# Spreading the scales 1/deviation by a turn on VectorE and transfers, and starting the seven-product form one chunk earlier

## The chip, the cores and the metric

The kernel runs on one core of a Trainium2 chip. The metric is the device time of one execution in microseconds. The kernel before has a median of 1026.7 us in three runs (1024.91, 1026.70 and 1027.67). PE is TensorE, DVE is VectorE, ACT is ScalarE, POOL is GpSimd, and SP only issues transfers.

## The reference, cut to what matters

```python
x = A_q                                            # 1 x 2048 x 576
xn = (x - mean(x)) / sqrt(var(x) + 1e-5)           # over the 576 channels
kv = v * (causal convolution of k with 4 taps)     # per channel
y = (causal convolution of kv with ssm_k, 2048 long) + kv * ssm_D
out = x + xn * y + relu(xn @ w1) @ w2              # w1: 576 x 4608, w2: 4608 x 576
```

The last term is the feed-forward part, and most of the work. The long convolution is done as a transform, a product and a transform back.

## The kernel before

**Chunks.** The feed-forward part takes the tokens in two halves of 1024, and in each half the 4608 hidden channels in 18 chunks of 256: 36 chunks in all, numbered g = 0 to 35. In a chunk the 1024 tokens are two blocks b = 0, 1 of 512, and the 256 hidden channels are two groups f = 0, 1 of 128. A chunk has a first part, relu(xn @ w1), which goes to the tiles psh, and a second part, which multiplies the hidden values of the chunk before by w2 in eight **units** (`open_unit` and `mm2`, 128 tokens each) into the tiles pso. There are two pso buffers, and a unit can only begin when DVE has added the unit before the last to acc (line 748 or 752). Each value is kept as a high and a low part (`hh` and `ll`, or index 0 and 1 of an operand) and a product is done as high times high, high times low and low times high: three matmuls for each 128 channels.

**Two forms of the first part.** In the plain form (`classical`) each of the four pairs (b, f) takes 12 matmuls for 512 of the 576 channels and two for the remaining 64: 56 matmuls of 128x512 per chunk. In the seven-product form (`quad`) sums of operands and of weights replace one of eight block products: seven products of six matmuls, and four times two for the remaining 64 channels, so 50. Its operands are called, in the order in which `quad` uses them, 00, 01, s2, s1, s3, s4 and 11; the remaining channels are hl0 and hl1. `PLAIN = 3`: chunks 0 to 2 are plain, chunk 3 is the first with seven products. In `quad` the order on PE is: product 00, units 0 and 1, product 01 and hl0, unit 2, s2, unit 3, s1, unit 4, s3, hl0, s4, units 5 and 6, hl1, unit 7, 11, hl1. After s4, DVE adds `u2` (line 686), ACT then refills a psh buffer (line 688), and the matmuls of hl1 wait for that.

**The start.** The plain chunks use operands that are centred but not divided by the deviation, and DVE multiplies a unit's result by rstd, which is 1/deviation (line 748). The seven-product chunks use operands that are already scaled. For them each block needs rstd as a row over its 512 tokens, the same on all 128 partitions (`row[b]`). The kernel before makes diagonal matrices from rstd on DVE (`diagonal`, eight instructions), multiplies them on PE by a matrix of ones (`scales`, line 327, one matmul in full float32 for each block) and copies the result out on ACT (line 330).

**Pieces.** With the rows there, `second_half_of_start` is a generator of pieces: `scaled` multiplies an operand by its row (line 340, DVE), `combined` takes differences of operands (line 227, DVE), and `made` splits an operand into its high part (line 212, ACT) and its low part (line 213, DVE). A piece is put into the program behind each unit (`post(1)`) and behind each `classical` (`post(3)`). The yields "00" and "10" are barriers, since the new operands overwrite those that the plain form still reads. If `quad` comes to an operand that isn't made yet, `need` puts the missing pieces there, right ahead of the product. `here()` orders a piece behind the newest addition to acc and the newest hh that were written before it.

**What sets the order.** PE follows the order in which its instructions are written. DVE and ACT run in one fixed order each, which a scheduler has set at build time within the orders that the code asks for; on the chip an engine does not pass over an instruction that waits. The long convolution's work is a second stream (`conv`), whose steps `tick` deals out between the feed-forward's matmuls by a budget: `rate` comes from `FFN_TOTAL`, which counts the chunks after the plain ones, and the stream begins when the pool of the start closes, after the first seven-product chunk. In its stage of products, a product reads psf on DVE (line 1051), sends parts through a transfer, and the next `join` (line 1063) waits for that transfer.

Of the kernel before, what the change touches and what calls it, by code (L numbers as in the profile page):

```python
# [10 lines left out]
F32 = mybir.dt.float32  # L11
F32R = mybir.dt.float32r
AF = mybir.ActivationFunctionType
OP = mybir.AluOpType
# [3 lines left out]
P = 128  # L18
# [28 lines left out]
W_MM = 512  # L47
W_UNIT = 2 * FT * 3 * NH
PAUSE = 16000
PLAIN = 3  # L50
PAUSES = 7.5
SHARE = 0.935

# [46 lines left out]
def h3_ffn_kernel(ctx: ExitStack, tc, x, k, v, shift_k, ssm_k, ssm_D, w1, w2, fwd, inv, mid, out):  # L100
# [27 lines left out]
    rows_n = dram.tile([HB, BT // 2, 2, P, D], F32, name="rows_n")  # L128
    ops_n = {o: dram.tile([P, 2, 2, 512], F32, name=f"ops_{o}") for o in OPERANDS}
    hl_n = dram.tile([HB, P, 512], F32, name="hl_n")  # L130

    def at_t(z, t):

# [6 lines left out]
    def fft_psum():  # L140
        return ps_f.tile([P, 512], F32, tag="f", name="psf")
# [170 lines left out]

    row = {}

    def diagonal(pool, b):
        diag = pool.tile([P, 2, D], F32, tag="xn", name=f"diag{b}", bufs=4)
        diag = diag[:, 0, :BT * P].rearrange("p (i n) -> p i n", i=BT)
        for i in range(BT):
            nc.vector.tensor_scalar(diag[:, i, :], ident, rstd[:, b * BT + i:b * BT + i + 1],
                                    None, op0=OP.mult)  # L320
        return diag

    def scales(pool, b, diag):

        ps = fft_psum()
        with tc.issue_after(done["pe"].ins):
            done["pe"] = nc.tensor.matmul(ps, ones, diag.rearrange("p i n -> p (i n)"),
                                          start=True, stop=True)
        row[b] = pool.tile([P, 512], F32, tag=f"row{b}", name=f"row{b}")
        nc.scalar.activation(row[b], ps, AF.Copy)  # L330

    def scaled(o, b):
        if isinstance(o, int):
# [18 lines left out]
    def made_rest(b):  # L352
        with here():
            split_rest(rest_operand(b), xf[b])
        ready.add(b)
        yield

    def combined(pool, o):
        for c in range(2):
            with here():  # L360
                combine(pool, xf, (o,), c)
            yield

    def second_half_of_start(pool):


        for o, b in (("11", 1), ("10", 1), ("00", 0), ("01", 0)):
            yield from scaled(o, b)
        for o in ("s1", "s2"):
            yield from combined(pool, o)  # L370
            yield from made(o)
        yield from combined(pool, "s3")
        yield from made("s3")
        yield from scaled(0, 0)
        yield "00"
        yield from made("00")
        yield from made("01")
        yield from made_rest(0)
        yield from combined(pool, "s4")
        yield from scaled(1, 1)  # L380
        yield "10"
        yield from made("s4")
        yield from made_rest(1)
        yield from made("11")
# [826 lines left out]
    load_acc(BT + 2)  # L1211
    for j in range(FT):
        load_w2(0, j)
    ones = const.tile([P, P], F32, name="ones")
    nc.vector.memset(ones, 1.0)
    table = const.tile([P, 1], F32, name="table")
    nc.vector.memset(table, 1.0)
    nc.scalar.activation(table, table, AF.Sqrt)
# [8 lines left out]
    with tc.tile_pool(name="fa", bufs=1) as fa:  # L1227
        block_xT(fa, 0, ("00", "01"), (None, None), block_rows(fa, 0))
        xn = block_rows(fa, 1)
        classical(0, 0, 0, 1)  # L1230
        classical(0, 0, 1, 2)
        block_xT(fa, 1, ("10", "11"), ("s4", None), xn)
        load_w1(1)
        with tc.issue_after(done["low"].ins):
            inv_std(0, 2 * BT)
        with tc.issue_after(done["centred"].ins):
            for j in range(FT):
                split_w2(0, j)
                load_w2(1, j)
        classical(0, 1, 0, 0)  # L1240
        split_a(1)
        classical(0, 1, 1, 0)
        split_r(1)
        split_b(1)
        split_d(1)
        load_w1(2)
        diag = {b: diagonal(fa, b) for b in (1, 0)}

        def unit(g, b, i, upto):
            open_unit(g, b, i)  # L1250
            mm2(g, b, i)
            post(1, upto)

        for g in range(1, PLAIN):
            now = "00" if g < PLAIN - 1 else "10"
            for f in range(FT):
                for i in range(2):
                    unit(g - 1, 0, 2 * f + i, "00")
                if g == 1:
                    scales(fa, 1 - f, diag[1 - f])  # L1260
                if g == f == 1:
                    posts["at"] = second_half_of_start(fa)
                classical(g, 0, f, 0, 3, now if f else "00")
            for j in range(FT):
                split_w2(g, j)
                load_w2(g + 1, j)
            for i in range(BT):
                unit(g - 1, 1, i, now)
            classical(g, 1, 0, 0, 3, now)
            split_a(g + 1)  # L1270
            if g + 1 == PLAIN:
                sums(g + 1)
            split_r(g + 1)
            classical(g, 1, 1, 0, 3, None if g == PLAIN - 1 else now)
            split_b(g + 1)
            split_d(g + 1)
            load_w1(g + 2)
        quad(PLAIN, [(PLAIN - 1, b, i) for b in range(2) for i in range(BT)])
        post(99)
# [36 lines left out]
```

## Time and profile before

| what | value |
|---|---|
| runs | 1024.91, 1026.70, 1027.67 us |
| span of the profiled execution | 1026.2 us (0.5 below the median; the page gives no other time of it) |
| mean granted TensorE clock | 0.998 |
| DVE busy | 709.2 us (69%) |
| ACT busy | 429.7 us (42%) |
| POOL busy | 486.8 us (47%) |
| DMA | mean 180 GB/s |

A PE matmul counts as busy from its start to its modelled end, and the next one starts before that end. What a matmul takes of the span is therefore read from the starts: 12 matmuls of 128x512 begin over 2.75 us, and the twelve of a unit (288 columns) over 1.59 us.

### The profile page before, as it was taken

To read this page: it belongs to the slowest core of one execution; us is meant where nothing else is said; L and a number is where in the kernel's file an instruction comes from. 1 tells how busy PE (TensorE), PEld (TensorE's weight loads), DVE (VectorE), ACT (ScalarE), POOL (GpSimd) and SP (SyncE) were. 2 spreads that over 40 slices of the span, in tenths; PEclk is the share of its full clock that TensorE was granted. 3 is DMA by queue.
4 is the path that set the end of the run, shared out by engine and by line. 5 is a ranking of instruction groups with operands and counts; after the bars stand their busy time and mean duration, and the time that the engine had idled before them with its cause. 6 is when DMAs were issued, how large, how long until landed. Compare 5 with 4: busy or idle time off the path is not lost.

```text
span 1026.2 us, 17380 instructions
## 1 busy us (share of the span) xinstructions
PE 1011.8 (99%) x6506; PEld 845.9 (82%) x6506; DVE 709.2 (69%) x1075; ACT 429.7 (42%) x761; POOL 486.8 (47%) x532
## 2 busy tenths in 40 slices
PE   9999999999999999999999999989999999999997
PEld 5898999998988889888878889867767777788777
DVE  6787677776465567779787889456656676656765
ACT  7244334443344444444434444444535355332220
POOL 4335446659544557555545455414423344344450
PEclk9999999999999999999999999999999999999999
DMA  7114467558245565369943433677778887857784
GB/s 177 48 44 117 116 173 168 181 175 200 73 134 174 179 196 146 112 208 370 277 139 125 137 97 115 205 222 222 228 227 245 236 264 238 225 189 238 207 256 116
DMA packets 92249, 184.70 MB, mean 180 GB/s; under 512 B 32082, under 2 KB 44500, under 8 KB 91268
## 3 DMA queue, kind: packets, MB, share of 16 engines
q1 hardware_dynamic: 73588, 123.47, 39.8%
q0 software_dynamic: 18256, 59.22, 20.0%
q10 hardware_dynamic: 320, 0.88, 0.3%
q8 instruction: 51, 0.84, 0.3%
q14 instruction: 34, 0.28, 0.1%
HBM read 119.04 MB, written 45.61 MB: 160 GB/s over the span
## 4 chain that ended last, share of the span: by engine, by line
PE 87%; DVE 4%; POOL 2%; DMA 2%; issue 2%; ACT 1%; SPq 1%; DVEq 0%; POOLq 0%; ACTq 0%
PE pso L571 40%; PE psh L571 34%; PE psf L765 5%; PE psg L765 4%; PE psh_c L571 3%; DMA area<-area 1%; POOL area L812 1%; PE psw L1223 1%; DMA r<-in_w 1%; DVE area L944 1%; DVE area L1051 1%; DVE area L945 0%; SPq L1029 0%; DVE sums L527 0%; DVE x L295 0%
## 5 line engine op out<-in xcount | busy, mean ns | idle before, releaser
L571 PE MATMUL pso<-w,hh 128*128 128x288 f32 x2304 | 468.4, 297 | 0.0
L571 PEld LDWEIGHTS pso<-w,hh 128*128 128x128 f32 x2304 | 378.6, 188 | 34.8 <-issue 15.6
L571 PE MATMUL pso<-w,ll 128*128 128x288 f32 x1152 | 340.0, 295 | 0.0
L752 DVE TENSOR_TENSOR acc<-pso,acc 128x576 f32<-128x576 f32 x243 | 183.0, 754 | 157.4 <-PE pso L571 157.1
L571 PEld LDWEIGHTS pso<-w,ll 128*128 128x128 f32 x1152 | 216.8, 188 | 0.0
L515 POOL TENSOR_TENSOR wb<-sums,wb 128x512 fp32r<-128x512 f32 x33 | 51.2, 1552 | 236.1 <-ACT wb L514 208.5
L515 POOL TENSOR_TENSOR w<-r,w 128x576 fp32r<-128x576 f32 x72 | 107.8, 1505 | 106.9 <-ACT w L514 105.8
L571 PE MATMUL psh<-x,wa 128*128 128x512 f32 x396 | 102.9, 395 | 0.5 <-POOL wa L515 0.3
L571 PE MATMUL psh<-xs,wb 128*128 128x512 f32 x396 | 102.0, 393 | 0.0
L571 PE MATMUL psh<-hl,wr 128*128 128x512 f32 x264 | 85.9, 407 | 6.3 <-ACT psh L688 6.3
L571 PEld LDWEIGHTS psh<-x,wa 128*128 128x128 f32 x396 | 72.3, 188 | 16.1 <-POOL wa L515 0.8
L571 PEld LDWEIGHTS psh<-xs,wb 128*128 128x128 f32 x396 | 70.8, 188 | 11.4
L515 POOL TENSOR_TENSOR wa<-r,wa 128x512 fp32r<-128x512 f32 x36 | 53.7, 1490 | 52.8 <-ACT wa L514 52.8
L595 DVE SCALAR_TENSOR_TENSOR ll<-psh,hh 128x512 fp32r<-128x512 f32 x66 | 45.2, 685 | 40.9 <-ACT hh L593 40.7
L688 ACT ACTIVATE psh<-psh 128x512 f32<-128x512 f32 x33 | 19.2, 582 | 128.2 <-DVE u L686 128.2
L571 PEld LDWEIGHTS psh<-hl,wr 128*128 128x128 f32 x264 | 46.0, 188 | 27.1 <-issue 13.2
L765 PE MATMUL psf<-area 64*64 64x512 f32 (+10 forms) x592 | 61.1, 473 | 0.0
L593 ACT ACTIVATE hh<-psh 128x512 fp32r<-128x512 f32 x66 | 39.4, 597 | 49.7 <-PE psh L571 49.0
L765 PE MATMUL psg<-area 64*64 64x512 f32 (+10 forms) x568 | 55.3, 453 | 0.0
L593 ACT ACTIVATE hh<-p 128x512 fp32r<-128x512 f32 x33 | 20.9, 632 | 79.1 <-DVE p L693 43.2
L1024 ACT ACTIVATE area<-psg 128x1024 f32<-128x1024 f32 x34 | 33.2, 1025 | 48.7 <-PE psg L765 48.1
L1051 DVE TENSOR_TENSOR area<-psf,area 128x512 f32<-128x512 f32 x72 | 44.7, 681 | 9.4 <-DMA area<-area 6.7
(140 smaller groups left out, 1525.1 us busy)
## 6 DMA issues: line engine op xcount, KB each, us to landing
r<-in_w POOLq DMA_DIRECT2D x70, 288.0 KB, 3.4
area<-area SPq DMA_DIRECT2D x144, 128.0 KB, 3.8
r<-in_w POOLq DMA_DIRECT2D x35, 512.0 KB, 5.1
zk<-area SPq DMA_DIRECT2D x64, 144.0 KB, 2.3
area<-zk SPq DMA_DIRECT2D x18, 512.0 KB, 4.5
area<-zx SPq DMA_DIRECT2D x18, 512.0 KB, 3.9
zy<-area SPq DMA_DIRECT2D x18, 512.0 KB, 4.8
area<-zy SPq DMA_DIRECT2D x32, 288.0 KB, 5.4
```

The source lines that it names most:

```text
L515: nc.gpsimd.tensor_tensor(w[:, 1, :n], src, w[:, 0, :n], OP.subtract)
L571: last = nc.tensor.matmul(ps, a, m, start=start and n == 0, stop=n == len(seq) - 1, skip_group_check=True)
L593: done["act"] = nc.scalar.activation(hh, ps, AF.Relu)
L595: nc.vector.scalar_tensor_tensor(ll, ps, 0.0, hh, op0=OP.max, op1=OP.subtract)
L688: nc.scalar.activation(x, y, AF.Copy, scale=-1.0)
L752: done["acc"] = nc.vector.tensor_tensor(two(acc[t]), ps[:, :, :NH], two(acc[t]), OP.add)
L765: done["pe"] = nc.tensor.matmul(ps, a, m, start=start, stop=stop, skip_group_check=True)
L812: nc.gpsimd.dma_start(kt[halves(h)[0], d:d + KD, :], src)
L944: nc.vector.tensor_tensor(e, win[t - n], sk[:, n, :], OP.mult)
L1024: nc.scalar.activation(dst, src, AF.Copy)
L1051: nc.vector.tensor_tensor(filt[c][:, k, :], banks[k], filt[c][:, k, :], OP.mult)
L1223: last = nc.tensor.matmul(idle[0], warm[:, :P], warm, start=True, stop=True)
```

## The change

```diff
-PLAIN = 3
+PLAIN = 2
...
+    scale_n = dram.tile([2 * BT, P], F32, name="scale_n")
...
-    def diagonal(pool, b):
-        diag = pool.tile([P, 2, D], F32, tag="xn", name=f"diag{b}", bufs=4)
-        diag = diag[:, 0, :BT * P].rearrange("p (i n) -> p i n", i=BT)
-        for i in range(BT):
-            nc.vector.tensor_scalar(diag[:, i, :], ident, rstd[:, b * BT + i:b * BT + i + 1],
-                                    None, op0=OP.mult)
-        return diag
-
-    def scales(pool, b, diag):
-
-        ps = fft_psum()
-        with tc.issue_after(done["pe"].ins):
-            done["pe"] = nc.tensor.matmul(ps, ones, diag.rearrange("p i n -> p (i n)"),
-                                          start=True, stop=True)
-        row[b] = pool.tile([P, 512], F32, tag=f"row{b}", name=f"row{b}")
-        nc.scalar.activation(row[b], ps, AF.Copy)
+    def spread_scales(pool):
+
+        sq, turned = (pool.tile([P, 32], F32, tag=f"sq{n}", name=f"sq{n}") for n in range(2))
+        nc.vector.tensor_copy(sq, rstd[:, :2 * BT].unsqueeze(1).to_broadcast([P, 4, 2 * BT]))
+        nc.vector.transpose(turned, sq)
+        for q in range(P // 32):
+            queue = nc.scalar if q % 2 else nc.sync
+            queue.dma_start(scale_n[:, 32 * q:32 * q + 32], turned[32 * q:32 * q + 2 * BT])
+        for b in (0, 1):
+            row[b] = pool.tile([P, 512], F32, tag=f"row{b}", name=f"row{b}")
+            src = scale_n[b * BT:(b + 1) * BT].rearrange("(o i) p -> o (i p)", o=1)
+            nc.sync.dma_start(row[b], src.to_broadcast([P, 512]))
...
-        for o, b in (("11", 1), ("10", 1), ("00", 0), ("01", 0)):
+        for o, b in (("00", 0), ("11", 1), ("10", 1), ("01", 0)):
             yield from scaled(o, b)
-        for o in ("s1", "s2"):
-            yield from combined(pool, o)
-            yield from made(o)
-        yield from combined(pool, "s3")
-        yield from made("s3")
+        yield from combined(pool, "s1")
+        yield from combined(pool, "s2")
+        yield from made("s2")
         yield from scaled(0, 0)
         yield "00"
         yield from made("00")
         yield from made("01")
         yield from made_rest(0)
+        yield from made("s1")
+        yield from combined(pool, "s3")
+        yield from made("s3")
         yield from combined(pool, "s4")
         yield from scaled(1, 1)
         yield "10"
...
-    ones = const.tile([P, P], F32, name="ones")
-    nc.vector.memset(ones, 1.0)
...
-        diag = {b: diagonal(fa, b) for b in (1, 0)}
+        spread_scales(fa)
...
-                if g == 1:
-                    scales(fa, 1 - f, diag[1 - f])
-                if g == f == 1:
+                if g == 1 and not f:
                     posts["at"] = second_half_of_start(fa)
```

Chunk 2 now has the seven-product form, and the pieces begin half a chunk earlier. The rows come by a copy and a turn of 32x32 blocks on DVE, four small writes to DRAM (two from SP, two from ACT) and two reads of 256 KB that spread a row over 128 partitions. The program moves in three places that matter below. In the rows, an operand's name is followed by a number of the build.

The first place is DVE at unit 4 of the first seven-product chunk. Before, this was chunk 3, and all its operands but one had long been made:

```order
L748 SCALAR_TENSOR_TENSOR acc4_115<-pso2_4_1019,rstd_84,acc4_115 128x576
L527 TENSOR_TENSOR sums4_1065<-r1_4_927 128x256 x2
L527 TENSOR_TENSOR sums4_1065<-sums4_1065,r1_4_927 128x256 x2
L686 TENSOR_TENSOR u2_3_1017<-psh3_5_1033,u2_3_1017 128x512
L748 SCALAR_TENSOR_TENSOR acc4_115<-pso2_5_1045,rstd_84,acc4_115 128x576
```

Now it is chunk 2, and between unit 4's addition to acc and `u2` DVE has this (xf10 and xf01 become s3 and s4 in place, xs3 and xs4 are the split operands):

```order
L746 SCALAR_TENSOR_TENSOR acc4_116<-pso1_4_773,rstd_84,acc4_116 128x576
L228 TENSOR_TENSOR xf10_333<-xf10_333,xf00_230 128x512 x2
L525 TENSOR_TENSOR sums3_828<-r1_3_678 128x256 x2
L228 TENSOR_TENSOR xf01_232<-xf01_232,xfs2_595 128x512 x2
L332 TENSOR_TENSOR xfr1_337<-xfr1_337,row1_436 64x512
L214 TENSOR_TENSOR xs3_817<-xf10_333,xs3_817 128x512
L525 TENSOR_TENSOR sums3_828<-sums3_828,r1_3_678 128x256
L214 TENSOR_TENSOR xs3_817<-xf10_333,xs3_817 128x512
L214 TENSOR_TENSOR xs4_843<-xf01_232,xs4_843 128x512 x2
L525 TENSOR_TENSOR sums3_828<-sums3_828,r1_3_678 128x256
L684 TENSOR_TENSOR u2_2_771<-psh2_5_789,u2_2_771 128x512
```

The whole making of s3 and s4 has moved here, behind the addition of the unit that PE does right ahead of product s3.

The second place is ACT from the last hidden values of chunk 1 on, as it now stands (hh1_1_1 is the high part of the last plain product of chunk 1, x00 and x01 are operands of chunk 2):

```order
L591 ACTIVATE hh1_1_1_663<-psh1_c11_648 128x512
L213 ACTIVATE x00_667<-xf00_230 128x512 x2
L512 ACTIVATE wb2_672<-sums2_640 128x512
L512 ACTIVATE wd2_675<-r1_2_422 128x256
L213 ACTIVATE x01_706<-xf01_232 128x512
L512 ACTIVATE wc2_709<-sums2_640 128x512
L213 ACTIVATE x01_706<-xf01_232 128x512
L209 ACTIVATE hl0_734<-xfr0_234 64x512
```

Before, x00 stood behind hh2_0_1 of a plain chunk, a block and a half ahead of the chunk that reads it; now it stands right behind the product that PE does last ahead of product 00.

The third place is late in the program, on DVE ahead of `u2` of chunk 25, in the convolution's stage of products. Before:

```order
L1051 TENSOR_TENSOR area_1173<-psf_7048,area_1173 128x512 x2
L1051 TENSOR_TENSOR area_1173<-psf_7049,area_1173 128x512 x2
L752 TENSOR_TENSOR acc12_5207<-pso24_12_7027,acc12_5207 128x576
L527 TENSOR_TENSOR sums26_7128<-r1_26_6898 128x256 x2
L527 TENSOR_TENSOR sums26_7128<-sums26_7128,r1_26_6898 128x256
L1063 SCALAR_TENSOR_TENSOR area_1173<-area_1173,sign_85 128x1024
L527 TENSOR_TENSOR sums26_7128<-sums26_7128,r1_26_6898 128x256
L1051 TENSOR_TENSOR area_1173<-psf_7101,area_1173 128x512
L1051 TENSOR_TENSOR area_1173<-psf_7102,area_1173 128x512
L1051 TENSOR_TENSOR area_1173<-psf_7101,area_1173 128x512
L1051 TENSOR_TENSOR area_1173<-psf_7102,area_1173 128x512
L686 TENSOR_TENSOR u2_25_7025<-psh25_5_7041,u2_25_7025 128x512
```

And now:

```order
L1049 TENSOR_TENSOR area_952<-psf_7027,area_952 128x512 x2
L750 TENSOR_TENSOR acc10_5169<-pso24_10_7005,acc10_5169 128x576
L593 SCALAR_TENSOR_TENSOR ll25_0_0_7056<-psh25_1_6978,hh25_0_0_7055 128x512
L750 TENSOR_TENSOR acc10_5169<-pso24_11_7059,acc10_5169 128x576
L750 TENSOR_TENSOR acc12_5255<-pso24_12_7086,acc12_5255 128x576
L1061 SCALAR_TENSOR_TENSOR area_952<-area_952,sign_85 128x1024
L525 TENSOR_TENSOR sums26_7160<-r1_26_6922 128x256 x2
L1049 TENSOR_TENSOR area_952<-psf_7133,area_952 128x512 x2
L525 TENSOR_TENSOR sums26_7160<-sums26_7160,r1_26_6922 128x256
L1049 TENSOR_TENSOR area_952<-psf_7134,area_952 128x512 x2
L525 TENSOR_TENSOR sums26_7160<-sums26_7160,r1_26_6922 128x256
L684 TENSOR_TENSOR u2_25_7084<-psh25_5_7100,u2_25_7084 128x512
```

Before, one unit's addition stood between a product and the next join ahead of `u2`; now three units' additions stand between them. Chunk 28 stands as chunk 25 does now. In chunk 30 a join ahead of `u2` follows two units behind a product, and before that was so in chunk 27.

## The prediction

> **What bounds the kernel now.** First the page's busy times and its chain of work that ended last.
>
> ```profile
> span 1026.2 us, 17380 instructions
> PE 1011.8 (99%) x6506; PEld 845.9 (82%) x6506; DVE 709.2 (69%) x1075; ACT 429.7 (42%) x761; POOL 486.8 (47%) x532
> PE 87%; DVE 4%; POOL 2%; DMA 2%; issue 2%; ACT 1%; SPq 1%; DVEq 0%; POOLq 0%; ACTq 0%
> ```
>
> PE is busy throughout and carries 87% of the chain. So a matmul less is time won, and what DVE, ACT and transfers do counts only where PE must stand for it. The view of who waits for whom, for PE, has one entry over 2 us:
>
> ```profile
> PE psh L571 <- ACT psh L688: 6.3, 3, 2.7
> ```
>
> Then the timeline of PE at the start, for what a matmul costs. I read starts, since the durations overlap.
>
> ```profile
> 32.38 0.29 PE L571 MATMUL pso<-w,ll 128*128 128x288 f32 x1
> 32.97 1.12 PE L327 MATMUL psf<-diag,ones 128*128 128x512 f32 x2 [0.29 <-DVE diag L319]
> 33.53 3.33 PE L571 MATMUL psh_c<-x,wa 128*128 128x512 f32 x12
> 36.70 0.62 PE L571 MATMUL psh_c<-hl,wr 128*128 128x512 f32 x2
> ...
> 40.34 1.02 PE L327 MATMUL psf<-diag,ones 128*128 128x512 f32 x2
> ...
> 42.58 1.54 PE L571 MATMUL psh_c<-x,wd 128*128 128x512 f32 x6
> ...
> 50.78 2.92 PE L571 MATMUL psh_c<-x,wa 128*128 128x512 f32 x12
> 53.53 0.62 PE L571 MATMUL psh_c<-hl,wr 128*128 128x512 f32 x2
> 53.99 1.53 PE L571 MATMUL psh_c<-x,wb 128*128 128x512 f32 x6
> 55.36 1.53 PE L571 MATMUL psh_c<-x,wd 128*128 128x512 f32 x6
> ...
> 57.20 0.43 PE L571 MATMUL pso<-w,hh 128*128 128x288 f32 x2
> ...
> 60.38 2.93 PE L571 MATMUL psh_c<-x,wa 128*128 128x512 f32 x12
> ```
>
> Twelve matmuls of 128x512 take 53.53 - 50.78 = 2.75 us, so 0.23 each; a product of six takes 1.4; two units take 60.38 - 57.20 = 3.18, so 1.59 each.
>
> **What goes.** The matmuls of ones: the first group of twelve begins 0.13 after 32.38 at best, at 32.51, and its successor at 36.70, which is 4.19 instead of 2.75: 1.44 us, of which 0.29 was a wait for DVE. The second time, 40.34 to 42.58 is 2.24 where 53.99 to 55.36 was 1.37: 0.87. Together **-2.3 us**. The seven-product form of chunk 2 drops 6 of 56 matmuls: 6 x 0.23 = **-1.4 us**. The memset of ones, eight DVE instructions for the diagonals and two ACT copies go too; PE stands behind none of them beyond the 0.29.
>
> **The rows by transfers.** The rows for this, of POOL, of DVE and of the transfers (KB each, and the median us to landing):
>
> ```profile
> 32.94 0.78 POOL L496 DMA_DIRECT2D r<-in_w  x1 [0.30 <-POOL wd L515]
> 30.77 3.03 DVE L319 TENSOR_SCALAR diag<-ident,rstd 128x128 f32<-128x128 f32 x8
> 147.45 0.70 DVE L452 STREAM_TRANSPOSE area<-area 128x512 f32<-128x512 f32 x1
> zk<-area SPq DMA_DIRECT2D x64, 144.0 KB, 2.3
> area<-area SPq DMA_DIRECT2D x144, 128.0 KB, 3.8
> hl<-hl_n SPq DMA_DIRECT2D x2, 256.0 KB, 9.9
> ```
>
> The copy takes the place of the diagonals at 30.77, the turn stands behind unit 0's addition and ends near 32.1 (at most 0.7 for it, by the larger turn above). A row needs a write and, after it, a read. No row has such small writes: I take 2.3 for the write, 0.6 for the second issue on its queue and 3.8 for the read, so the row lands at 38.8. By the lowest row for both it is 36.7, by the highest for the read 44.9. DVE's first scaling comes after the addition of unit 2 (near 38.2 without the ones). Behind it on DVE are unit 3's addition, five more scalings, a low part and unit 4's addition, which ends near 45.2, while PE wants that pso buffer for unit 6 at 45.3. So lateness goes straight to PE: **+0.5 us**, bounds 0 and 6.6. ACT issues two of the writes, but has no work then before the next hh.
>
> **Operands that are made too late.** This is the largest term. The steps from PE to ACT and DVE, in the timelines of the same stage:
>
> ```profile
> 46.00 0.43 PE L571 MATMUL pso<-w,hh 128*128 128x288 f32 x2
> 46.20 0.82 DVE L748 SCALAR_TENSOR_TENSOR acc<-pso,rstd,acc 128x576 f32<-128x576 f32 x1 [0.20 <-PE pso L571]
> 57.40 0.60 ACT L593 ACTIVATE hh<-psh_c 128x512 fp32r<-128x512 f32 x1 [1.72 <-PE psh_c L571]
> 57.89 1.15 ACT L212 ACTIVATE xs<-xfs 128x512 fp32r<-128x512 f32 x2
> 58.03 0.69 DVE L595 SCALAR_TENSOR_TENSOR ll<-psh_c,hh 128x512 fp32r<-128x512 f32 x1 [2.45 <-ACT hh L593]
> 58.64 0.68 DVE L213 TENSOR_TENSOR xs<-xfs,xs 128x512 fp32r<-128x512 f32 x1
> 59.24 0.81 DVE L748 SCALAR_TENSOR_TENSOR acc<-pso,rstd,acc 128x576 f32<-128x576 f32 x1
> 59.97 0.74 DVE L227 TENSOR_TENSOR xfs<-xf,xfs 128x512 f32<-128x512 f32 x1
> 80.50 0.74 DVE L527 TENSOR_TENSOR sums<-r 128x256 f32<-128x256 f32 x2
> 81.17 0.41 DVE L527 TENSOR_TENSOR sums<-sums,r 128x256 f32<-128x256 f32 x1
> 84.85 0.62 ACT L514 ACTIVATE wb<-sums 128x512 fp32r<-128x512 f32 x1
> 85.37 0.41 ACT L514 ACTIVATE wd<-r 128x256 fp32r<-128x256 f32 x1
> ```
>
> DVE and ACT begin 0.20 after PE has passed on; ACT's copies follow each other by 0.5; a low part begins 0.63 after its high part; DVE's operations of 512 columns follow by 0.61 and last 0.68, additions by 0.73, a pair of sums by 0.67. Now the order of the changed program, place by place, counted from the end of what PE did last:
>
> - 00, from the end of the last plain product: hh at 0.20, x00 high at 0.7 and 1.2 (done 1.3 and 1.8), ll at 0.83, x00 low at 1.44 and 2.05 (done 2.1 and 2.7). PE's first matmul begins at 1.35, its second at 2.15, its sixth ends at 3.3 instead of 1.4: 1.9.
> - 01, from the end of 00: the second half's low part stands behind unit 1's addition, at 3.18 + 0.20 + 0.73 = 4.11, done 4.8; wanted at 3.18 + 4 x 0.23 = 4.1: 0.7. hl0's low part follows and costs 0.15.
> - s1: the same with unit 3: 0.7.
> - s3, from the end of unit 4: addition at 0.20, differences at 0.93 and 1.54, two sums at 2.15, two differences for s4 at 2.82 and 3.43, xfr1 at 4.04, the first low part at 4.65 (done 5.3), a sum, the second at 5.6 (done 6.3). ACT's high part is there at 2.2. PE does one matmul at 2.2, the next at 5.35, ends at 6.75 instead of 1.4: **5.35**.
> - hl1, from the end of s4: unit 5's addition at 1.79, ll, hl1 low at 3.13 (done 3.8), wanted at 3.18: 0.65. Then 11: on DVE, unit 6's addition at 3.74, x11's first low part at 4.47 and p5 at 5.08 (done 5.8). On ACT follow hh of p5 and three splits of the next weights (0.5, 0.5, 0.3, 0.3) ahead of x11's second high part, done near 8.0; its low part is done at 8.8. PE wants the high part at 6.6 and ends at 9.25 instead of 7.3: 1.95.
>
> That makes **+11.4 us**. Each place starts from PE itself, so an early or late start of the chunk doesn't change it. Before, the same pieces lay behind units of plain chunks, whose matmuls wanted none of them. The lower bound of a place is 0 (if an engine passes over what waits, which no row shows), the upper one perhaps a quarter more: 0 to 14.
>
> **The clock.** A long wait has a second price. By stretches, of PE alone, with its granted clock behind the busy time:
>
> ```profile
> 517.60:521.00 3.40, 1.45 (x11) 1.00 0.48 158
> 521.00:524.40 3.40, 3.40 (x14) 0.50 0.28 81
> 684.80:690.00 5.20, 2.51 (x20) 1.00 0.92 306
> ```
>
> Behind the wait of 2 us near 519 the clock was halved for 3.4 us; behind one of 2.7 near 689 it was not. In s3 PE has one matmul in over 5 us, so I count one such stretch, half of 3.4: **+1.7 us**, bounds 0 and 5.1 (three stretches). The Trainium skill, "TensorE: Matmul & The Clock Gate", section "HAM oscillation — how this bites in real kernels", warns only of gaps over some 3.4 us; by it s3's longest gap of 2.9 would cost no clock and the sum would be 1.7 lower. The trace, with its halving after 2 us, speaks against it.
>
> **The later stages.** The budget of the convolution's stream changes little, but its pieces fall elsewhere. The three waits of 6.3 us and the halved clock cost 8.0 us now. What made the longest:
>
> ```profile
> 683.73 1.29 DVE L1063 SCALAR_TENSOR_TENSOR area<-area,sign 128x1024 f32<-128x1024 f32 x1 [2.07 <-DMA area<-area]
> 686.20 2.48 DVE L1051 TENSOR_TENSOR area<-psf,area 128x512 f32<-128x512 f32 x4 [0.84 <-DMA area<-area]
> 688.60 0.68 DVE L686 TENSOR_TENSOR u<-psh,u 128x512 f32<-128x512 f32 x1
> ```
>
> A join close behind a product waits for its transfer, and `u2` stands behind it. Two of the three waits were of this kind; in the changed order one place (chunk 30) is as close, and chunks 25 and 28 have more units in between. I keep one such wait and one of another kind, 2 x 2.1 = 4.2: **-3.8 us**, bounds -8.0 and +3.
>
> **Sum.** 1026.2 - 2.3 - 1.4 + 0.5 + 11.4 + 1.7 - 3.8 = 1032.3; the median stands 0.5 above this span, so **1032.8 us**.
>
> **Rivals.** (1) *The late stage pays for the start*: none of the later waits comes back, -8.0 instead of -3.8, so 1028.6, no difference that can be told (0.3% is about what a measurement of this kernel can tell from no change, 1023.6 to 1029.8). It decides at chunks 25, 28 and 30 in `u2`: if the transfers land before the join there, PE doesn't stand. For it: more units in between. Against it: chunk 30. (2) *The order hides more than I count*, the waits of chunk 2 shrink to 3 us and no clock is lost: 1032.8 - 8.4 - 1.7 = 1022.7, faster. Against it: the order on DVE is fixed, and s3 alone has ten instructions between unit 4 and its second low part. (3) *Worse*: rows 3 us late, three halved stretches, no gain later: 1032.8 + 2.5 + 3.4 + 3.8 = 1042.5. For it: POOL sets off the load of chunk 2's weights at 32.9, so the rows' transfers share the engines with it.
>
> **Chances.** Forecast, 1030 to 1038: 0.63. Rival 1: 0.15, of which a fifth ends above 1029.8. Rival 2: 0.07, of which a third only reaches no change. Rival 3: 0.15. The range 1026 to 1040 leaves out rival 2 and two thirds of rival 3, 0.17. Faster 0.05, same 0.14, slower 0.81.
>
> **What would show it.** In the profile after: no L327; PE's waits for x00, x01, s1, s3, hl1 and x11 between 55 and 90 us, the longest at s3 near 2.9; a halved clock there; a unit of chunk 0 waiting near 45 if the rows are late; three or fewer waits at `psh` for line 686. The prediction is wrong if PE passes s3 without a wait of over 2 us, or if more than 8 us of waits leave or enter the later stages.

## The result, and the profile after

The changed kernel takes 1040.0 us (median of 4 runs, 1038.68 to 1041.20) where the kernel before takes 1026.9 on the same chip: a ratio of 1.0127, with a 95% interval of 1.0113 to 1.0141. It is slower, by 13 us. The forecast was 1032.8, so the direction is right and the size is not: the median lies 0.02 us above the upper end of the range, 1026 to 1040.

The page of the changed kernel, with its span, its busy times and the chain that ended last:

```profile
span 1039.4 us, 17405 instructions
PE 1015.3 (98%) x6496; PEld 846.1 (81%) x6496; DVE 713.2 (69%) x1073; ACT 433.3 (42%) x766; POOL 494.0 (48%) x533
PE 89%; DVE 5%; DMA 2%; issue 1%; ACT 1%; SPq 1%; ACTq 0%; DVEq 0%
```

PE has ten matmuls fewer and yet 3.5 us more of busy time. Matmuls that last longer are a sign of the clock, not of more work: the mean granted clock is 0.991, where it was 0.998. The view of who waits for whom, for PE:

```profile
PE psh L569 <- DVE xs L214: 4.5, 2, 2.5
PE psh L569 <- ACT psh L686: 3.9, 2, 2.1
PE psh L569 <- ACT x L213: 2.9, 2, 1.6
PE psh L569 <- ACT xs L213: 2.2, 1, 2.2
PE psh L569 <- DVE x L214: 1.3, 3, 0.6
...
PE psh L569 <- DVE hl L210: 0.6, 1, 0.6
```

Lines 213 and 214 are the high and low parts of operands, 210 the low part of `hl`. Of these lines only the entry of line 686 was there before (as line 688, 6.3 in three), and its two waits lie late in the program; the others lie in chunk 2. Where, shows the timeline of PE. Each row is a run of matmuls, with the wait ahead of it in brackets:

```profile
54.25 0.62 PE L569 MATMUL psh_c<-hl,wr 128*128 128x512 f32 x2
56.14 0.50 PE L569 MATMUL psh<-x,wa 128*128 128x512 f32 x1 [1.26 <-ACT x L213]
...
63.06 0.74 PE L569 MATMUL psh<-x,wa 128*128 128x512 f32 x2 [0.59 <-DVE x L214]
...
68.93 1.09 PE L569 MATMUL psh<-xs,wc 128*128 128x512 f32 x4
72.01 0.85 PE L569 MATMUL psh<-xs,wc 128*128 128x512 f32 x2 [1.99 <-DVE xs L214]
...
77.92 0.50 PE L569 MATMUL psh<-xs,wb 128*128 128x512 f32 x1 [2.17 <-ACT xs L213]
80.93 2.50 PE L569 MATMUL psh<-xs,wb 128*128 128x512 f32 x5 [2.51 <-DVE xs L214]
```

What a wait costs I read from starts, as in the prediction. At s1 four matmuls begin at 68.93 and the next could at 68.93 + 4 x 0.23 = 69.85; it begins at 72.01, 2.16 later. Read so, chunk 2 loses 2.0 at 00, 0.75 at 01, 2.2 at s1, 5.1 at s3 (the matmul ahead of it ran at half clock and counts twice its time), 0.8 at hl1 and 2.4 at 11: **13.2 us** where the forecast had 11.4.

The last plain product ends at 54.25 + 2 x 0.23 = 54.7, against 57.20 before: 2.5 us gained by then.

The other price is the clock. The busy time by stretches of 3.41 us, with the granted clock behind POOL's entry:

```profile
55.40:58.82 3.42, 2.38 (x11) 1.85 (x12) 1.89 (x3) 3.42 (x8) 2.33 (x4) 1.00 0.00 0
...
69.06:72.47 3.41, 1.42 (x7) 0.85 (x6) 2.82 (x2) 0.00 (x0) 2.88 (x4) 1.00 0.32 89
72.47:75.88 3.41, 3.28 (x14) 2.82 (x12) 0.10 (x1) 0.60 (x1) 0.00 (x0) 0.50 0.29 87
75.88:79.30 3.42, 0.50 (x1) 0.19 (x1) 3.42 (x7) 1.42 (x3) 0.00 (x0) 1.00 0.00 0
79.30:82.71 3.41, 1.78 (x4) 1.49 (x5) 3.41 (x7) 1.04 (x2) 0.00 (x0) 0.50 0.00 0
82.71:86.12 3.41, 3.41 (x9) 2.64 (x8) 0.64 (x2) 0.00 (x0) 0.00 (x0) 0.50 0.00 0
92.95:96.36 3.41, 1.42 (x5) 0.63 (x5) 2.07 (x3) 2.00 (x5) 2.46 (x2) 1.00 0.00 0
96.36:99.78 3.42, 3.42 (x10) 2.63 (x9) 0.69 (x1) 1.11 (x2) 3.11 (x6) 0.50 0.76 190
...
864.36:867.78 3.42, 3.42 (x18) 0.79 (x17) 1.96 (x3) 0.85 (x3) 0.00 (x0) 0.50 0.71 163
```

Four stretches of chunk 2 ran at half clock. PE was busy in them for 3.28 + 1.78 + 3.41 + 3.42 = 11.9 us, half of which is lost: **5.9 us**, where the forecast had one stretch and 1.7. So chunk 4 begins 15.0 us late. The start of its first product in PE's timeline, before and after:

```profile
107.71 1.54 PE L571 MATMUL psh<-x,wa 128*128 128x512 f32 x6
122.76 1.54 PE L569 MATMUL psh<-x,wa 128*128 128x512 f32 x6
```

From there to the end it is 916.6 us instead of 918.5, 1.9 less, where the forecast had 3.8.

### The profile page after: what moved, and what is told of

Its sections match the earlier page's. It is cut to its first block, busy times and chain, and to the rows that moved or that the text cites. A ratio compares the mean times of both kernels' runs of the same rounds, so it can differ in the third digit from the quotient of the medians.

```text
span 1039.4 us, 17405 instructions
## 1 busy us (share of the span) xinstructions
PE 1015.3 (98%) x6496; PEld 846.1 (81%) x6496; DVE 713.2 (69%) x1073; ACT 433.3 (42%) x766; POOL 494.0 (48%) x533
## 4 chain that ended last, share of the span: by engine, by line
PE 89%; DVE 5%; DMA 2%; issue 1%; ACT 1%; SPq 1%; ACTq 0%; DVEq 0%
PE pso L569 41%; PE psh L569 37%; PE psf L763 5%; PE psg L763 4%; DMA area<-area 2%; PE psh_c L569 1%; DVE area L1049 1%; PE psw L1219 1%; DVE ll L593 1%; DVE xf L337 0%; DMA row<-scale_n 0%; SPq L1054 0%; DVE acc L746 0%; DVE x L296 0%; PE psx L234 0%
## 5 line engine op out<-in xcount | busy, mean ns | idle before, releaser
L569 PEld LDWEIGHTS pso<-w,hh 128*128 128x128 f32 x2304 | 379.2, 188 | 32.4 <-issue 13.2
L750 DVE TENSOR_TENSOR acc<-pso,acc 128x576 f32<-128x576 f32 x250 | 188.6, 755 | 154.7 <-PE pso L569 153.9
L569 PE MATMUL psh<-xs,wb 128*128 128x512 f32 x408 | 106.6, 396 | 4.7 <-DVE xs L214 2.5
L569 PE MATMUL psh<-x,wa 128*128 128x512 f32 x408 | 107.3, 398 | 2.7 <-ACT x L213 1.3
L569 PE MATMUL psh<-hl,wr 128*128 128x512 f32 x272 | 89.9, 412 | 4.5 <-ACT psh L686 3.9
L569 PEld LDWEIGHTS psh<-x,wa 128*128 128x128 f32 x408 | 75.3, 190 | 19.8 <-ACT x L213 1.7
L569 PEld LDWEIGHTS psh<-xs,wb 128*128 128x128 f32 x408 | 73.5, 189 | 17.2 <-DVE xs L214 2.8
L513 POOL TENSOR_TENSOR wa<-r,wa 128x512 fp32r<-128x512 f32 x36 | 57.8, 1607 | 48.0 <-ACT wa L512 48.0
L684 DVE TENSOR_TENSOR u<-psh,u 128x512 f32<-128x512 f32 x34 | 23.5, 690 | 48.1 <-PE psh L569 47.8
L569 PE MATMUL psh<-xs,wc 128*128 128x512 f32 x204 | 53.1, 394 | 2.4 <-DVE xs L214 2.0
L569 PE MATMUL psh<-x,wc 128*128 128x512 f32 x204 | 53.4, 395 | 2.0 <-ACT x L213 1.6
```

The source lines that it names most:

```text
L513: nc.gpsimd.tensor_tensor(w[:, 1, :n], src, w[:, 0, :n], OP.subtract)
L569: last = nc.tensor.matmul(ps, a, m, start=start and n == 0, stop=n == len(seq) - 1, skip_group_check=True)
L684: nc.vector.tensor_tensor(u2, x, u2, OP.add)
L750: done["acc"] = nc.vector.tensor_tensor(two(acc[t]), ps[:, :, :NH], two(acc[t]), OP.add)
```

## The experiments

All ratios are to the kernel before on the same chip, with 95% intervals. "Waits" are PE's losses at the operands of chunk 2, from starts. "Half clock" counts the stretches of 3.41 us between 50 and 105 us in the profile, "chunk 4" is the start of its first product, "rest" what follows to the end of the span.

| kernel | median us | ratio | waits | half clock | chunk 4 | rest |
|---|---|---|---|---|---|---|
| before | 1026.4 to 1027.0 | 1 | 0 | 0 | 107.7 | 918.5 |
| changed | 1040.0 | 1.0127 [1.0113, 1.0141] | 13.2 | 4 | 122.8 | 916.6 |
| e1_plain3 | 1028.9 | 1.0020 [1.0006, 1.0034] | - | 0 | 107.6 | 918.7 |
| e2_post3 | 1028.7 | 1.0018 [1.0005, 1.0031] | 5.4 | 0 | 110.9 | 919.2 |
| e3_fill | 1037.7 | 1.0114 [1.0087, 1.0140] | filled | 0 | 118.8 | 916.5 |
| e4_ones | 1043.1 | 1.0164 [1.0139, 1.0189] | 13.2 | 5 | 126.9 | 916.9 |
| e5_again | 1038.9 | 1.0118 [1.0102, 1.0134] | 13.0 | 5 | 123.6 | 913.8 |
| e6_pool | 1040.4 | 1.0134 [1.0117, 1.0150] | 14.6 | 3 | 123.3 | 916.8 |
| e7_early | 1024.3 | 0.9980 [0.9971, 0.9989] | 2.0 | 0 | 106.2 | 916.4 |
| e8_old_order | 1036.5 | 1.0107 [1.0088, 1.0125] | 10.8 | 2 | 119.1 | 919.3 |
| e9_rows | 1029.6 | 1.0031 [1.0019, 1.0043] | - | 0 | 108.1 | 922.5 |
| e10_plain3_early | 1035.7 | 1.0089 [1.0068, 1.0111] | - | 1 | 114.4 | 921.6 |
| e11_plain3_pool | 1032.8 | 1.0050 [1.0029, 1.0070] | - | 2 | 112.2 | 917.8 |
| e12_fill_more | 1038.4 | 1.0104 [1.0086, 1.0123] | filled | 0 | 118.2 | 920.2 |
| e13_after_more | 1041.5 | 1.0141 [1.0121, 1.0161] | 13.2 | 4 | 123.0 | 915.7 |

All columns behind the ratio come from one profiled execution of each kernel. Some of these took 2.5 to 3.8 us more than the kernel's median (e2 3.2, e4 2.5, e8 3.8, e9 2.7), and the three profiles of the changed kernel (changed, e5, e13) have 916.6, 913.8 and 915.7 in the last column. Differences of some 3 us there tell nothing of a kernel.

**e1_plain3**: the changed kernel with the form's old place.

```diff
-PLAIN = 2
+PLAIN = 3
```

> The changed kernel with PLAIN = 3 again: rows by the turn and transfers, pieces reordered and begun early, but chunk 2 plain. Theory (waits in a chunk 2 whose operands are made too late, and the clock halved behind them, are the whole loss): no wait over 1 us on PE between 50 and 100 us, no halved clock there, and the two matmuls of ones are saved, so 1024.5 us (1022.5 to 1026). Rival (the rows by transfers or the new order of the pieces cost time by themselves): 1030 or more, with PE waiting near 45 us.

Without the seven-product form in the third chunk the loss of 13 us is nearly gone. The gain over the kernel before is not there: 1028.9 lies above the theory's range and below the rival's. In the profile the same plain product begins 1.75 us earlier than before at 49.0 us and 0.24 earlier at 76.3; between them a unit waits 1.35 for an addition. e9 to e11 follow that up.

**e2_post3**: more pieces behind each unit of chunk 2.

```diff
-            post(1)
+            post(3 if g == PLAIN else 1)
```

> The changed kernel with three pieces instead of one behind each unit of chunk 2, so that s1, s3, s4 and 11 are made ahead of the unit before their product. Theory: the waits at s1, s3 and 11 go, the halved clock with them, those at 00 (2 us) stays; 1040 less 2 + 5.3 + 2.4 + 6 is 1024 us (1022 to 1028). Rival (DVE has no room for the pieces in chunk 2, whatever their order): the waits move to the units, 1035 or more. Rival (the loss lies in the later stages): 1036 or more.

Posting alone takes 11 us back, to 0.7 us above the range. The waits at s1 and 11 are gone, most of that at s3 too, and with the idle time the halved clock. Left are 2.0 at 00, 1.7 at 01, 0.9 at s3 (which the expectation of e7_early calls s2) and 0.8 at hl1.

**e3_fill**: matmuls of zeros, whose results nobody reads, in the waits at s1, s3 and 11 (36 in all).

```diff
...
+                if o == "s3" and c == 0:
+                    fill(10)
+                    matmuls(ps, seq[:1], s0)
+                    seq, s0 = seq[1:], False
+                    fill(11)
+                elif c == 1 and o in ("s1", "11"):
+                    fill(8 if o == "s1" else 7)
...
```

> The changed kernel with 36 matmuls of zeros (bf16, 512 columns, into a free psf buffer) in the waits at s1, s3 and 11, short enough to fit into them. Theory (the clock is halved because PE stood still, and that costs 6 us beside the waits): granted clock 1.0 from 55 to 100 us, waits unchanged, 1034 us (1032 to 1036.5). Rival (the halving comes from something else, or costs little): the clock rows stay halved, 1040 or more.

No halved clock is left in the profile, and chunk 4 begins 4.0 us earlier. The median of 4 runs, spread over 5 us, was above what I expected and could not be told from the changed kernel's; hence e12 and e13.

**e4_ones**: the rows by two matmuls of ones, both just ahead of the pieces; the rest of the change stays.

```diff
-        spread_scales(fa)
+        diag = {b: diagonal(fa, b) for b in (0, 1)}
...
+                    for b in (0, 1):
+                        scales(fa, b, diag[b])
```

> The changed kernel with the rows by two matmuls of ones again, both right ahead of the pieces. Theory: the rows by transfers are a gain of about 2.3 us, less some 0.3 of a wait near 45 us: 1042 us (1040.5 to 1043.5). Rival (the transfers arrive late and cost more than the matmuls): 1039 or less.

The waits of chunk 2 are the same 13.2, chunk 4 begins 4.1 us later than in the changed kernel, some 1.6 of it by a fifth halved stretch. The other 2.5 stand already at the start of product 00: so much do the transfers spare the start, where the forecast had 2.3 less 0.5.

**e5_again**: the changed kernel, for a second profile.

> The changed kernel once more, unchanged, for a second profile of it. In the profiles so far every halved stretch of the granted clock is 3.41 us long and within one execution they lie on one grid of 3.413 us (72.47, 79.30, 96.36 and 864.36 us in the changed kernel: 2, 7 and 232 steps), and this grid lies otherwise in each execution. Theory: what halves the clock is the idle time of TensorE summed within one step of this grid (about 2.1 us or more of 3.41), not the length of one wait. Then this execution has the same waits of chunk 2 (2.0 at 00, 0.75 at 01, 2.2 at s1, 5.3 at s3, 0.8 at hl1, 2.4 at 11, each within 0.15), its halved stretches lie on a grid of another phase, each right behind a step with over 2.0 us idle, and their number in chunk 2 may be anything from 2 to 4. Rival: the length of a wait alone decides, and the halved stretches follow the same waits (s1, both at s3, 11) at the same places as before, 72.5, 79.3 to 86.1 and 96.4, whatever the phase. Time by both: 1040 us (1038.5 to 1041.5).

The gaps between PE's starts came out within 0.03 us of the first profile at all places, the halved stretches did not: they ran from 73.67 to 87.32 without a break, and from 97.56 to 100.97, five in all and one more than expected. That speaks for the theory. e13 decides it.

**e6_pool**: three of POOL's splits, and the loads behind two of them, moved away from s1's low parts in chunk 2.

```diff
-        split_w2(g, 0)
-        if more:
-            load_w2(g + 1, 0)
+        if g != PLAIN:
+            split_w2(g, 0)
+            if more:
+                load_w2(g + 1, 0)
...
-        if more:
+        if more and g != PLAIN:
             split_a(g + 1)
...
         unit(5)
+        if g == PLAIN:
+            split_a(g + 1)
+            for j in range(FT):
+                split_w2(g, j)
+                load_w2(g + 1, j)
...
```

(`split_w2(g, 1)` is changed as `split_w2(g, 0)` is.)

> The changed kernel, with three of GpSimd's low parts of weights (both of this chunk's second layer and the next chunk's wa) issued behind unit 5 of chunk 2 and no longer at 66 to 71.4 us, beside s1's low parts. Theory: those made VectorE's low part of s1 take 2.09 us in place of 0.68; without them it takes 0.7 to 0.85, the wait at s1 falls from 2.2 to about 0.75 us, and with so little idle time no halved stretch follows it: 1.4 us and at most 1.7 us less, 1038.0 us (1036.8 to 1039.2). Rival: the low part is long of itself or held up by something else (ScalarE's high part, the sequence), and stays at 2 us: 1040 us (1039 to 1041).

The rows of DVE and POOL at s1, in the timeline of the changed kernel:

```profile
66.33 1.43 POOL L513 TENSOR_TENSOR w<-r,w 128x576 fp32r<-128x576 f32 x1 [3.97 <-ACT w L512]
66.88 1.42 DVE L214 TENSOR_TENSOR xs<-xfs,xs 128x512 fp32r<-128x512 f32 x1
67.72 1.74 POOL L513 TENSOR_TENSOR wa<-r,wa 128x512 fp32r<-128x512 f32 x1
69.13 0.82 DVE L746 SCALAR_TENSOR_TENSOR acc<-pso,rstd,acc 128x576 f32<-128x576 f32 x1 [0.82 <-PE pso L569]
...
69.87 2.09 DVE L214 TENSOR_TENSOR xs<-xfs,xs 128x512 fp32r<-128x512 f32 x1
69.99 1.41 POOL L513 TENSOR_TENSOR w<-r,w 128x576 fp32r<-128x576 f32 x1
```

And in e6_pool, where POOL does nothing there but splits from 87 on:

```profile
67.35 0.68 DVE L214 TENSOR_TENSOR xs<-xfs,xs 128x512 fp32r<-128x512 f32 x1
...
70.33 0.68 DVE L214 TENSOR_TENSOR xs<-xfs,xs 128x512 fp32r<-128x512 f32 x1
...
88.47 3.26 POOL L513 TENSOR_TENSOR w<-r,w 128x576 fp32r<-128x576 f32 x2
...
90.50 1.79 DVE L214 TENSOR_TENSOR x<-xf,x 128x512 fp32r<-128x512 f32 x1
92.21 0.81 DVE L753 SCALAR_TENSOR_TENSOR acc<-pso,rstd,acc 128x576 f32<-128x576 f32 x1
92.94 1.51 DVE L593 SCALAR_TENSOR_TENSOR ll<-p,hh 128x512 fp32r<-128x512 f32 x1
94.37 2.02 DVE L214 TENSOR_TENSOR x<-xf,x 128x512 fp32r<-128x512 f32 x1
94.42 0.73 POOL L513 TENSOR_TENSOR wd<-r,wd 128x256 fp32r<-128x256 f32 x1
```

Both low parts of s1 fall to 0.68 and the wait there to 0.75: the mechanism is as the theory had it. The time is not, because the moved splits, and POOL's next ones behind them, now stand beside x11's low parts, which take 1.79 and 2.02; the waits at hl1 and 11 grow from 3.2 to 6.0.

**e7_early**: e2_post3, and a second piece behind each unit of block 1 in chunk 1.

```diff
             for i in range(BT):
                 unit(g - 1, 1, i, now)
+                post(1)
```

> The changed kernel with three pieces behind each unit of chunk 2 and, beside that, a second piece behind each of the four units of block 1 in chunk 1. Theory: the operands of chunk 2 are late only because too few pieces stand ahead of what VectorE waits for; with four more pieces ahead, 00's low parts stand in front of the last low part of chunk 1 and no longer behind it, the waits left by three pieces for each unit (2.0 at 00, 1.7 at 01, 0.9 at s2 and 0.8 at hl1, 5.4 us in all) fall to 1 us or less, and the time is 1024.3 us (1022.5 to 1026), below the kernel before. Rival: VectorE has no room in chunk 1; the accumulations and low parts behind the added pieces come late, TensorE waits for them for as long as it no longer waits for operands, and the time stays at 1028.7 us (1027.5 to 1030).

1024.3 us, as the theory had it, and the only kernel here that beats the kernel before: by 0.2%, with an interval that leaves 1 out. From its view of who waits for whom:

```profile
PE psh L569 <- ACT psh L686: 4.7, 4, 2.1
...
PE psh L569 <- POOL wa L513: 1.0, 1, 1.0
```

Lines 213, 214 and 210 are gone from the view. Left in chunk 2 are 1.2 us for the split of `wa` and 0.8 for the copy of line 686.

**e8_old_order**: the pieces in the order of the kernel before.

```diff
-        for o, b in (("00", 0), ("11", 1), ("10", 1), ("01", 0)):
+        for o, b in (("11", 1), ("10", 1), ("00", 0), ("01", 0)):
```

(and s1, s2 and s3 made ahead of `scaled(0, 0)`)

> The changed kernel with the pieces of the second half of the start in the order of the kernel before (s1, s2 and s3 made ahead of 00): the seven-product form from the third chunk and the rows by transfers alone. Theory: the order moves the waits and hardly their sum: those at s1 (2.2) and s3 (5.3) go, and 00 comes about five pieces later, some 3.5 to 4.5 us beside its 2.0, with one halved stretch behind it: 1035.5 us (1033 to 1038). Rival: the reordering is what makes the change bearable, since 00 comes so late that everything behind it is late too: 1043 us or more (1041 to 1047).

As expected within 1 us: 6.0 us lost at 00, nothing at s1 and s3, 10.8 in all. The reordering of the change moves the waits and doesn't shorten their sum.

**e9_rows**: e8_old_order with `PLAIN = 3`, so of the change the rows alone, and with them the earlier start of the pieces.

> Of the change only the rows by the turn and transfers, with what goes with them (the pieces may begin two units earlier): the seven-product form from the fourth chunk and the pieces in their order before. Theory: the four matmuls of ones (2.3 us with what stood around them) are gone, VectorE's four scalings of the identity too, nothing new waits, and what the first experiment lost again was lost by its order of pieces, not by the rows: 1024.3 us (1023 to 1025.5). Rival: 1026.4 us as before (1025.8 to 1027.2), since VectorE's work, or a wait in a unit of chunk 2, sets the pace of the start there whatever TensorE saves.

A miss: 1029.6. The rival was right that a unit of chunk 2 sets the pace, but part of the loss is later: from chunk 4 on the profiled execution takes 922.5 us, 4.0 more than before, of which up to 2.7 belong to this execution and not to the median. (The matmuls of ones are two, with two records each in the trace, and the scalings of the identity eight, not four of each.) The wait of 1.35 at 74.8 stands behind these rows of DVE, with POOL's beside them:

```profile
71.47 2.52 DVE L214 TENSOR_TENSOR x<-xf,x 128x512 fp32r<-128x512 f32 x2
73.91 0.81 DVE L745 SCALAR_TENSOR_TENSOR acc<-pso,rstd,acc 128x576 f32<-128x576 f32 x1
...
71.72 3.54 POOL L512 TENSOR_TENSOR w<-r,w 128x576 fp32r<-128x576 f32 x2 [10.37 <-ACT w L511]
```

**e10_plain3_early**: e7_early with `PLAIN = 3`.

> The best kernel so far (three pieces behind a unit, a second piece behind the units of block 1), but with the seven-product form from the fourth chunk. Theory: the form in the third chunk is worth its six matmuls, 1.4 us, and costs the 2.0 us of waits that are left in it; later stages give one or two us by where they fall: the two are equal within 1.5 us, 1024.5 us (1023 to 1026). Rival: the third chunk's form carries the whole gain over the kernel before, and without it the time is 1026.4 or more (1026 to 1028).

A miss too, by 11 us. In its timeline, of DVE and POOL:

```profile
92.17 1.39 POOL L513 TENSOR_TENSOR wc<-sums,wc 128x512 fp32r<-128x512 f32 x1
92.44 4.74 DVE L214 TENSOR_TENSOR x<-xf,x 128x512 fp32r<-128x512 f32 x2
93.53 1.42 POOL L513 TENSOR_TENSOR w<-r,w 128x576 fp32r<-128x576 f32 x1
94.92 1.71 POOL L513 TENSOR_TENSOR wa<-r,wa 128x512 fp32r<-128x512 f32 x1
...
97.09 0.80 DVE L746 SCALAR_TENSOR_TENSOR acc<-pso,rstd,acc 128x576 f32<-128x576 f32 x1
```

Two low parts of x11 take 4.74 us beside three of POOL's splits, an addition stands behind them, and PE waits 3.4 us for it at 97.95, with a halved stretch. What the form in the third chunk is worth by itself isn't settled by this.

**e11_plain3_pool**: e1_plain3, with POOL's splits of w2 in chunk 2 behind the first group of block 1.

```diff
+            if g > 1:
+                for j in range(FT):
+                    split_w2(g, j)
+                    load_w2(g + 1, j)
```

(The same lines ahead of block 1's units stand under `if g == 1` now.)

> The first experiment (seven-product form from the fourth chunk, rows by transfers, the new order of pieces) with GpSimd's low parts of w2 of chunk 2 issued behind the first matmul group of block 1 and no longer ahead of its units. Theory: the 1.35 us that TensorE waited at 74.59 us for an accumulation was a low part of an operand ahead of it on VectorE, which took 1.92 us beside GpSimd's split; with the split elsewhere it takes 0.68, that wait goes, and the time is 1.3 us below the first experiment's, which was 1.002 of the kernel before: 1027 us (1026 to 1028), with less than 0.4 us lost at that unit in the profile. Rival: the wait stays at the unit, and the time with it: 1028.5 us (1027.8 to 1029.5).

The wait at the unit fell from 1.35 to 0.7 and no further, and the kernel became slower: POOL is now late with `wa` of chunk 3, for which PE waits 3.0 us at 85.6, with two halved stretches.

**e12_fill_more** and **e13_after_more**: e3_fill and the changed kernel side by side.

> The filled waits once more, in more rounds and on the same chip as the changed kernel, for the price of the clock in the median rather than in one profile. Theory: in the changed kernel's profile four halved stretches of 3.41 us in chunk 2 hold 11.9 us of TensorE's work and cost half of it, 5.9 us; with the waits filled chunk 2 ended 4.0 us earlier in the profile (some of the zeros come in the way of real matmuls). How many stretches an execution has depends on where its grid lies, so the median moves by 3 to 5 us: 1035.5 us (1034.5 to 1037), and in the profile no halved stretch between 50 and 105 us. Rival: the profile of the first look was a lucky one, the zeros delay as much as the clock returns, and the two kernels are equal within 1 us: 1038.5 us (1037.5 to 1040).

> The changed kernel beside it, for the same comparison: 1039.5 us (1038.5 to 1040.5) by both theories, with two to five halved stretches in chunk 2, each behind a step of the grid with over 2 us idle, and the waits of chunk 2 within 0.15 us of the two profiles so far.

The medians differ by 3.1 us (5 runs each), as the theory had it, but both lie 2 to 3 us above what was expected, the filled kernel's within the rival's range, and the intervals of the ratios touch. In the profiles chunk 4 begins 4.9 us earlier with the filled waits, and the rest takes 4.5 more: two long waits at line 686 (702 in this kernel; 2.3 and 3.3) with a halved stretch behind each. So filling the waits saves 4.0 (e3) and 4.9 us of chunk 2, where the halved stretches cost 5.9 and 5.7. In e12's execution nearly all of it is lost again later, in e3's (rest 916.5) none; what the clock costs in the median is not shown more closely than the 3.1. The stretches of e13_after_more on its own grid:

```profile
55.32:58.74 3.42, 1.85 (x8) 1.25 (x8) 1.89 (x3) 3.26 (x7) 2.33 (x3) 1.00 0.00 0
58.74:62.15 3.41, 3.41 (x16) 3.41 (x15) 0.33 (x1) 1.76 (x4) 3.41 (x5) 0.50 0.00 0
...
72.39:75.80 3.41, 1.75 (x11) 1.66 (x12) 1.61 (x1) 0.60 (x1) 1.61 (x2) 1.00 0.50 128
75.80:79.22 3.42, 1.06 (x6) 0.52 (x4) 2.81 (x6) 1.23 (x2) 0.00 (x0) 1.00 0.11 44
```

Here the 2.0 us at 00 fall into one step, and a halved one follows; in the first profile they lay in two steps and none followed. The 2.2 us at s1, halved in the first profile, are shared here by two steps, and 75.80 runs at full clock.

## Why the prediction was right in direction and too small

| step | forecast | measured |
|---|---|---|
| matmuls of ones | -2.3 | -2.5 at the last plain product, rows included |
| six matmuls fewer | -1.4 | not told apart |
| rows by transfers | +0.5 | 0.3 |
| 00 / 01 and hl0 / s1 | 1.9 / 0.85 / 0.7 | 2.0 / 0.75 / 2.2 |
| s3 / hl1 / 11 | 5.35 / 0.65 / 1.95 | 5.1 / 0.8 / 2.4 |
| clock in chunk 2 | +1.7 | 5.9 |
| later stages | -3.8 | -1.9 (-4.7 and -2.8 in e5 and e13, the same kernel) |

With the -1.4 taken as forecast, the measured terms make -2.5 - 1.4 + 13.2 + 5.9 - 1.9 = 13.3, and the spans differ by 13.2. Of the 7.2 us by which the median is above the forecast, the clock makes 4.2, the waits 1.8 (1.5 of them at s1), and in this profile the later stages 1.9; the start gave 0.7 more than forecast.

- **The rows** came about as forecast: the writes had landed by 33.3, where the reads were issued, the reads took 4.6 us, the first scaling begins at 37.97, and PE lost 0.3 us at 45, where a unit wants the buffer. The gain is real only where nothing downstream eats it (e4 against e9).
- **The operands**: counting DVE's and ACT's rows from PE's last step gave four of six places to 0.25 us. That they are a matter of how many pieces stand ahead, and not of the engines' speed, show e2 and e7: the same operations posted earlier take 7.8 and 11.2 us of waits away, and DVE has room for them.
- **s1** is the one place that was mis-sized as a mechanism: 0.68 was taken for a low part wherever it stands. Beside POOL's splits it took 1.42 and 2.09, without them 0.68 (e6).
- **The clock** is the step that failed: "I count one such stretch, half of 3.4: **+1.7 us**, bounds 0 and 5.1 (three stretches)". That a wait halves the clock behind it was right, the size was not. I weighed each wait by its own length and asked whether it was long enough. The runs show idle time summed in steps of a grid: s1's 2.2 us and 11's 2.4 us are enough if they fall into one step, s3's 5.1 us reach over two steps, and the second of them stays halved. Four or five stretches in each of three profiles, 5.9 us in the first, are what "bounds 0 and 5.1" should have covered. The Trainium skill, "TensorE: Matmul & The Clock Gate", section "HAM oscillation — how this bites in real kernels", warns only of gaps over some 3.4 us, and by it there would have been none at all, since the longest here is 2.8; the measurement decides.
- **The later stages** kept two waits at line 686, 3.9 us in all, where I kept two of 4.2. I forgot the clock behind them: the stretch at 864.36 costs 1.7, and 8.0 - 3.9 - 1.7 is 2.4, near the 1.9 that came. In e5 no stretch was halved late in the program, and the rest was 4.7 shorter than before: that this term was wrong isn't shown.
- **The rivals**: the third one (1042.5) is nearest in time, by its three halved stretches, but its late rows didn't come. Rival 1 asked for no waits left later, and two were left. Rival 2 became true only with other postings (e7).

What stays open: why the rest of the program takes between 913.8 and 922.5 us in kernels whose work there is the same, and 913.8 to 916.6 in three executions of one kernel. The entry at line 686 makes part of it; which shift of the stages makes it long wasn't settled, and it is as large as what e1, e9 and e11 were to tell.

## What to carry to other kernels

When a chunk with more operands is moved ahead, count for each product where its last operand stands in the queue of the engine that makes it; the remedy is to issue the pieces earlier, not in another order, and it was worth 15 us here. Price idle time of TensorE in windows, not wait by wait: two short waits in one window of 3.4 us cost as much clock as a long one. And before moving GpSimd's work to another time, look at what VectorE and TensorE want at that time: both such moves here (e6, e11) gave back elsewhere what they won.

## What the runs showed of the hardware

**The clock goes by a grid.** In each of the 15 profiles the halved stretches lie on one grid of 3.413 us, whose place differs from execution to execution. I summed TensorE's idle time between 47 and 108 us in each step of it (from the starts of matmuls, at 0.23 us for 512 columns and 0.13 for 288, twice that in a halved step). Of 243 steps at full clock, the 17 with 2.01 us idle or more were each followed by a halved one, and the 226 with 1.95 or less by none. Of 26 halved steps, the 9 with 0.90 or more idle were followed by another, the 17 with 0.70 or less were not. The Trainium skill, "TensorE: Matmul & The Clock Gate", section "Part 1: The HAM clock gate (the "warmup" mystery)", has this free-running window of 3413 ns, and the grid agrees; it gives no share of a window from which the clock falls, and here that is about 2.0 of 3.41 us.

**VectorE slows beside GpSimd only in some operations.** In the changed kernel's trace the nine single low parts of line 214 with no GpSimd subtraction beside them all took 0.68 us; of five with one, two took the same and three 0.86 to 2.09. The 250 additions of line 750, which read one operand from PSUM and one from SBUF, had a maximum of 0.76 us both alone (161) and beside GpSimd (89). The Trainium skill, "SBUF — State Buffer", section "Who interferes with whom", says that a VectorE instruction with two SBUF inputs contends with a GpSimd instruction that reads SBUF; the rows agree, and a low part has two such inputs.
